# A mixer kernel on one core: the low word of float64 weights is rounded to an integer by ScalarE and added to the high part as 32-bit integers on GpSimd

## Chip, cores, metric

The program runs on one core of a Trainium2 chip. The metric is device time in microseconds (us) of one execution; lower is better. Several executions are timed and their median is given.

## What is computed

The reference chains three blocks over a batch of 8, with 576 tokens and a width of 512:

```python
# 1. attention within chunks of 64 tokens (8 heads of 64)
scores = scale * np.matmul(q_c, k_c.transpose(0, 1, 2, 4, 3))
attn = softmax(scores)                       # with the row maximum taken off
x = np.matmul(attn, v_c)
# 2. a gated block
h = np.maximum(x @ w_in, 0.0)
u, v = h[..., :512], h[..., 512:]
v_s = np.einsum('ts,bsd->btd', w_spatial, layer_norm(v)) + b_spatial[None, :, None]
x = (u * v_s) @ w_out
# 3. a token mixer and a channel mixer
u = x + (np.maximum(x^T @ w_tok1, 0.0) @ w_tok2)^T
out = u + np.maximum(u @ w_ch1, 0.0) @ w_ch2
```

Activations are float32. The weights w_in, w_out, w_tok1, w_tok2, w_ch1 and w_ch2 arrive as float64, which no engine of the kernel computes in: the kernel reads each as a pair of 32-bit words and makes a float32 of it.

## The kernel before

**Stages.** The first block and the gated block run batch by batch on PE, the tensor engine. A hand-written list of words (FIRST for the first batch, STEADY for the six that follow, LAST for the eighth) gives the order of the steps; a word is a step and the number of its tile. The second stage (token and channel mixers, from about 520 us) has its own order and converts nothing. Every engine runs its instructions strictly in the order of the list; semaphores hold an instruction until what it reads is written and its buffer is free.

**A piece of a float64 weight** has up to 128 rows and 512 columns. It is loaded by the SP queue into `craw` (two buffers; `wu_raw` for four pieces), as 32-bit words, the low word first and the high word second, so that each of them is read with a stride of 8 bytes. Then come three steps, words `wa`, `wm`, `we` for the twelve pieces of w_in and w_out in the first batch and `ca`, `cm`, `ce` for the 33 of the later weights:

- `conv_start` on ScalarE (ACT): the high word, read as a float32 and scaled, becomes `t` (tile `ctmp`, L143), and the low word, read as an integer, is scaled into a float32 in its own place (L144).
- `conv_mid` on VectorE (DVE): `t` is shifted left by three bits (L152), the sign is merged in (L154), and the power of two of the result is cut out into the place of the high word (L156).
- `conv_end` on GpSimd (POOL): low part times power of two (L164), and the product is added to `t` (L165).

After that the first twelve pieces are split into a rounded part (ACT, L187) and a rest (L190, on POOL or DVE), which the matrix products read. The 33 others are stored to memory by the SP queue (word `cs`, L215), which frees their buffers for the next loads (`cl`, L129).

**What stands around it in a steady batch.** The list has, in the early part: `x1 ca L2 S0 V0 s0 e0 ca n0 z0 cm ce V1 cm S1 R1 r1 R0 r0 ce T0 R2 r2 R3 r3 t0 V2 U0 s1 e1 P0 cs cs cl cl L3 x2 n1 z1 F G S2 ... T1`. In it `S` is the scores of a pair of heads on PE (L336), `s`, `e`, `n`, `z` their softmax (DVE L355 and L356, ACT L362, DVE L366 to L368, and the scaling on POOL, L372), `T` their transpose on PE (L380), `x` the transposes of q and k on DVE (L322, L323), `V` and `U` the product with w_in on PE (L479, L568), `R` ACT's evictions of V (L526) and `r` the batch-norm statistics on DVE (L531, L532). So two conversions stand ahead of the statistics on DVE, and behind those `s1`, `x2` and `n1`, before PE's `S2` and `T1`. Later in the batch `W` is the spatial product (L591, behind ACT's copy of the u half, L578), `D` copies the output projection out (ACT, L624) and stores it (SP, L625).

Of the kernel before, what the change touches and what calls it, by code (L numbers as in the profile page):

```python
# [10 lines left out]
U32 = mybir.dt.uint32  # L11
ACTF = mybir.ActivationFunctionType
ALU = mybir.AluOpType
# [42 lines left out]
def attention_gmlp_mixer(  # L56
# [15 lines left out]
    nc = tc.nc  # L72
# [4 lines left out]
    scale = 1.0 / float(D) ** 0.5  # L77

    def f32(ap):
        return ap.bitcast(F32)  # L80
# [34 lines left out]

    def conv_load(src, raw=None):

        nr, n = src.shape[0], src.free_size()  # L120
        if src.dtype == F32:
            raw = rp.tile([128, DM], F32, tag="ctmp", bufs=3, name="ctmp")[:nr, :n]
            nc.sync.dma_start(out=like(raw, src), in_=src)
            return raw
        if raw is None:
            raw = rp.tile([128, DM, 2], U32, tag="craw", bufs=2, name="craw")
        raw = raw[:nr, :n]
        src = src.bitcast(U32)
        nc.sync.dma_start(out=like(raw.rearrange("p n w -> p (n w)"), src), in_=src)  # L129
        return raw  # L130

    def like(ap, other):
        if len(other.shape) == 3:
            return ap.rearrange("p (g n) -> p g n", g=other.shape[1])
        return ap

    def conv_start(raw):
        if raw.dtype == F32:
            return raw, raw
        nr, n = raw.shape[:2]  # L140
        low, high = raw[:, :, 0], raw[:, :, 1]
        t = rp.tile([128, DM], F32, tag="ctmp", bufs=3, name="ctmp")[:nr, :n]
        nc.scalar.activation(out=t, in_=f32(high), func=ACTF.Copy, scale=2.0 ** -112)  # L143
        nc.scalar.activation(out=f32(low), in_=low, func=ACTF.Copy, scale=2.0 ** -52)  # L144
        return raw, t

    def conv_mid(raw, t):
        if raw.dtype == F32:
            return
        low, high = raw[:, :, 0], raw[:, :, 1]  # L150
        tu = t.bitcast(U32)
        nc.vector.tensor_scalar(  # L152
            out=tu, in0=tu, scalar1=3, scalar2=None, op0=ALU.logical_shift_left)
        nc.vector.scalar_tensor_tensor(  # L154
            out=tu, in0=high, scalar=0x80000000, in1=tu, op0=ALU.bitwise_and, op1=ALU.bitwise_or)
        nc.vector.tensor_scalar(  # L156
            out=high, in0=tu, scalar1=0xFF800000, scalar2=None, op0=ALU.bitwise_and)

    def conv_end(raw, t):

        if raw.dtype == F32:
            return raw
        low, high = raw[:, :, 0], raw[:, :, 1]
        nc.gpsimd.tensor_tensor(out=f32(high), in0=f32(low), in1=f32(high), op=ALU.mult)  # L164
        nc.gpsimd.tensor_tensor(out=t, in0=t, in1=f32(high), op=ALU.add)  # L165
        return t

    class Piece:
# [5 lines left out]
        def load(self, *a):  # L174
            self.x = conv_load(self.src, *a)

        def start(self):
            self.x = conv_start(self.x)

        def mid(self):  # L180
            conv_mid(*self.x)

        def end(self):
            self.x = conv_end(*self.x)
# [1150 lines left out]
```

## Time and profile before

| | us |
|---|---|
| median of 3 runs (lowest, highest) | 1257.33 (1256.14, 1257.96) |
| profiled execution | 1259.11 |
| its span, first to last instruction | 1257.3 |
| PE busy in the span | 1190.9 |
| DVE busy | 923.6 |
| ACT busy | 496.6 |
| POOL busy | 213.1 |

The span is that of the profiled execution; its time includes a little before the first and after the last instruction. Busy shares are averages over stages: PE is the busiest engine by far, and what an engine's waiting costs has to be read from the stage in which it waits. The rows below carry times in us from the start of the span.

### The profile page before, as it was taken

To read this page: it belongs to the slowest core of one execution; us is meant where nothing else is said; L and a number is where in the kernel's file an instruction comes from. 1 tells how busy PE (TensorE), PEld (TensorE's weight loads), DVE (VectorE), ACT (ScalarE), POOL (GpSimd) and SP (SyncE) were. 2 spreads that over 40 slices of the span, in tenths; PEclk is the share of its full clock that TensorE was granted. 3 is DMA by queue.
4 is the path that set the end of the run, shared out by engine and by line. 5 is a ranking of instruction groups with operands and counts; after the bars stand their busy time and mean duration, and the time that the engine had idled before them with its cause. 6 is when DMAs were issued, how large, how long until landed. Compare 5 with 4: busy or idle time off the path is not lost. (4 is left out here: it accounts for less than half of the span.)

```text
span 1257.3 us, 25171 instructions
## 1 busy us (share of the span) xinstructions
PE 1190.9 (95%) x9983; PEld 1123.0 (89%) x9983; DVE 923.6 (73%) x1427; ACT 496.6 (39%) x786; POOL 213.1 (17%) x205
## 2 busy tenths in 40 slices
PE   6689999999998999999889999999998999999997
PEld 4588998989797988898779899999998999999997
DVE  6897767687776868366686776767768977877786
ACT  2564535354544536244332332232225433333331
POOL 2644122222323231105220000000005100000000
PEclk9989999999999999999999999999999999999999
DMA  9956446374739383157545665565376576666663
GB/s 162 186 111 130 86 120 116 94 172 103 183 78 202 58 195 81 72 106 210 151 139 166 183 178 180 152 171 192 141 276 202 208 208 192 185 192 196 207 212 46
DMA packets 426362, 196.16 MB, mean 156 GB/s; under 512 B 369666, under 2 KB 389570, under 8 KB 426244
## 3 DMA queue, kind: packets, MB, share of 16 engines
q1 hardware_dynamic: 421380, 193.96, 58.9%
q8 instruction: 78, 1.28, 0.4%
q10 hardware_dynamic: 4864, 0.59, 0.3%
q14 instruction: 40, 0.33, 0.1%
HBM read 123.31 MB, written 71.17 MB: 155 GB/s over the span
## 5 line engine op out<-in xcount | busy, mean ns | idle before, releaser
L953 PE MATMUL ps_c<-ub,wt 128*128 128x288 f32 x2016 | 289.3, 299 | 7.8 <-DVE u L982 2.5
L953 PEld LDWEIGHTS ps_c<-ub,wt 128*128 128x128 f32 x2016 | 278.2, 191 | 14.0 <-ACT s L985 3.6
L953 PE MATMUL ps_c<-hb,wt 128*128 128x288 f32 x2016 | 269.1, 295 | 1.6 <-DVE hb L1042 1.5
L953 PEld LDWEIGHTS ps_c<-hb,wt 128*128 128x128 f32 x2016 | 268.2, 188 | 2.4 <-DVE hb L1042 2.3
L591 PE MATMUL ps_s<-ws,vn 128*128 128x288 f32 x768 | 110.9, 301 | 2.9 <-ACT ut L578 2.8
L1041 ACT CAST hb<-h 128x1728 fp32r<-128x1728 f32 x40 | 64.8, 1638 | 123.0 <-DVE h L1034 42.9
L591 PEld LDWEIGHTS ps_s<-ws,vn 128*128 128x128 f32 x768 | 105.9, 193 | 4.5 <-ACT ut L578 4.3
L617 PE MATMUL ps_o<-g,w_out 128*128 128x288 f32 x768 | 107.6, 297 | 0.7 <-DVE w_out L190 0.7
L568 PE MATMUL ps_u<-xt,w_in 128*128 128x288 f32 x768 | 107.9, 300 | 0.0
L568 PEld LDWEIGHTS ps_u<-xt,w_in 128*128 128x128 f32 x768 | 105.5, 193 | 0.9 <-POOL w_in L190 0.2
L617 PEld LDWEIGHTS ps_o<-g,w_out 128*128 128x128 f32 x768 | 102.6, 188 | 2.5 <-DVE w_out L190 0.9
L1042 DVE TENSOR_TENSOR hb<-h,hb 128x1728 fp32r<-128x1728 f32 x40 | 78.2, 1955 | 28.9 <-ACT hb L1041 28.9
L479 PE MATMUL ps_v<-w_in,xt 128*128 128x512 f32 x384 | 94.8, 404 | 2.7 <-ACT xt L423 1.3
L479 PEld LDWEIGHTS ps_v<-w_in,xt 128*128 128x128 f32 x384 | 72.8, 192 | 21.1 <-ACT xt L423 1.5
L372 POOL TENSOR_TENSOR e<-e,sm 128x512 f32<-128x512 f32 (+1 forms) x40 | 38.9, 972 | 226.9 <-DVE sm L368 153.7
L869 PE MATMUL ps_u<-w,h 128*128 128x288 f32 x384 | 61.8, 298 | 4.5 <-DVE xh L874 4.5
L910 ACT CAST ub<-xh 128x576 fp32r<-128x576 f32 x56 | 37.4, 672 | 70.0 <-DVE xh L917 66.8
L869 PEld LDWEIGHTS ps_u<-w,h 128*128 128x128 f32 x384 | 54.7, 190 | 5.7 <-DVE xh L874 5.6
L164 POOL TENSOR_TENSOR craw<-craw 128x512 f32<-128x512 f32 (+3 forms) x41 | 40.1, 978 | 116.0 <-DVE craw L156 34.0
L911 DVE TENSOR_TENSOR ub<-xh,ub 128x576 fp32r<-128x576 f32 x56 | 43.1, 770 | 21.1 <-ACT ub L910 20.6
L811 ACT CAST xn<-nat 128x512 fp32r<-128x512 f32 x40 | 24.8, 619 | 79.2 <-DVE nat L809 74.6
L830 PE MATMUL ps_h<-xn,w 128*128 128x512 f32 x192 | 51.2, 400 | 3.5 <-ACT xn L811 3.5
(145 smaller groups left out, 1697.9 us busy)
## 6 DMA issues: line engine op xcount, KB each, us to landing
hd<-c SPq DMA_DIRECT2D x120, 288.0 KB, 2.5
h<-hd SPq DMA_DIRECT2D x40, 864.0 KB, 6.7
craw<-in_moe_w_ch_dram SPq DMA_DIRECT2D x24, 512.0 KB, 4.8
x_raw<-x2d SPq DMA_DIRECT2D x160, 64.0 KB, 2.6
qk_raw<-in_q_dram SPq DMA_DIRECT2D x128, 72.0 KB, 4.2
qk_raw<-in_k_dram SPq DMA_DIRECT2D x128, 72.0 KB, 3.1
xh<-x2d SPq DMA_DIRECT2D x16, 576.0 KB, 5.6
u2d<-xh SPq DMA_DIRECT2D x16, 576.0 KB, 3.1
```

Source lines behind the costliest of these rows:

```text
L164: nc.gpsimd.tensor_tensor(out=f32(high), in0=f32(low), in1=f32(high), op=ALU.mult)
L372: nc.gpsimd.tensor_tensor(out=e, in0=e, in1=sm.to_broadcast([128, e.shape[1], 64]), op=ALU.mult)
L479: nc.tensor.matmul(ps, lhsT=self.xt[kc][:, p, 128 * ti:128 * ti + 128], rhs=w_in_t[r][:, kc, DM:2 * DM], start=kc == 0 and n == 0, stop=kc ...
L568: nc.tensor.matmul(ps[:, h, 0:HALF], lhsT=w_in_t[r][:, kc, 128 * m:128 * m + 128], rhs=self.xt[kc][:, p, HALF * h:HALF * h + HALF], start= ...
L591: nc.tensor.matmul(ps[:, h, 0:HALF], lhsT=lhsT, rhs=rhs[:, HALF * h:HALF * h + HALF], start=n == 0, stop=n == len(ops) - 1)
L617: nc.tensor.matmul(ps[:, h, 0:HALF], lhsT=w_out_t[r][:, kc, 128 * m:128 * m + 128], rhs=self.g[p][:, kc, h], start=kc == 0 and n == 0, sto ...
L830: nc.tensor.matmul(ps[kk], lhsT=PB["w1"][r][:, m, ksl], rhs=xn[:, p], start=m == 0 and n == 0, stop=False)
L869: nc.tensor.matmul(ps, lhsT=h1[:, kk, p, 128 * m:128 * m + 128], rhs=PB["w2"][r][:, kk, HALF * h:HALF * h + HALF], start=n == 0, stop=n == 5)
L911: eng.tensor_tensor(out=lo, in0=x, in1=f32(hi), op=ALU.subtract)
L953: nc.tensor.matmul(ps, lhsT=lhsT, rhs=rhs, start=first and n == 0, stop=n == len(ops) - 1, skip_group_check=True)
L1041: nc.scalar.copy(out=hi, in_=x)
L1042: nc.vector.tensor_tensor(out=lo, in0=x, in1=f32(hi), op=ALU.subtract)
```

## The change

ScalarE no longer scales the low word by 2^-52 into a float32: it scales it by 2^-29 and writes it back as a 32-bit integer, which is the number of units in the last place (0 to 8) that the low word adds to the high part's bits, rounded. DVE's third pass goes. On GpSimd the multiply goes, and in place of the float add an integer add of the bit patterns of `t` and the low word remains.

```diff
@@ conv_start
         nc.scalar.activation(out=t, in_=f32(high), func=ACTF.Copy, scale=2.0 ** -112)
-        nc.scalar.activation(out=f32(low), in_=low, func=ACTF.Copy, scale=2.0 ** -52)
+        nc.scalar.activation(out=low, in_=low, func=ACTF.Copy, scale=2.0 ** -29)
@@ conv_mid
         nc.vector.scalar_tensor_tensor(
             out=tu, in0=high, scalar=0x80000000, in1=tu, op0=ALU.bitwise_and, op1=ALU.bitwise_or)
-        nc.vector.tensor_scalar(
-            out=high, in0=tu, scalar1=0xFF800000, scalar2=None, op0=ALU.bitwise_and)
@@ conv_end
-        low, high = raw[:, :, 0], raw[:, :, 1]
-        nc.gpsimd.tensor_tensor(out=f32(high), in0=f32(low), in1=f32(high), op=ALU.mult)
-        nc.gpsimd.tensor_tensor(out=t, in0=t, in1=f32(high), op=ALU.add)
+        tu = t.bitcast(U32)
+        nc.gpsimd.tensor_tensor(out=tu, in0=tu, in1=raw[:, :, 0], op=ALU.add)
         return t
```

The order of all other instructions stays; the line numbers shift by one to two. On DVE, in a steady batch, from the first of the two conversions of the early part to the first statistics, the rows before are:

```order
L152 TENSOR_SCALAR ctmp<-ctmp 128x512
L154 SCALAR_TENSOR_TENSOR ctmp<-craw,ctmp 128x512
L156 TENSOR_SCALAR craw<-ctmp 128x512
L152 TENSOR_SCALAR ctmp<-ctmp 128x512
L154 SCALAR_TENSOR_TENSOR ctmp<-craw,ctmp 128x512
L156 TENSOR_SCALAR craw<-ctmp 128x512
L531 BN_STATS st<-v_5838 128x6
```

And now:

```order
L153 TENSOR_SCALAR ctmp<-ctmp 128x512
L155 SCALAR_TENSOR_TENSOR ctmp<-craw,ctmp 128x512
L153 TENSOR_SCALAR ctmp<-ctmp 128x512
L155 SCALAR_TENSOR_TENSOR ctmp<-craw,ctmp 128x512
L529 BN_STATS st<-v_5758 128x6
```

Two passes over 128x512 words are gone, and GpSimd's part of a piece now starts behind the second pass instead of the third. On POOL, the same place, from the softmax scaling of the first head pair to that of the second, before:

```order
L372 TENSOR_TENSOR e<-e,sm 128x512
L164 TENSOR_TENSOR craw<-craw 128x512
L165 TENSOR_TENSOR ctmp<-ctmp,craw 128x512
L164 TENSOR_TENSOR craw<-craw 128x512
L165 TENSOR_TENSOR ctmp<-ctmp,craw 128x512
L372 TENSOR_TENSOR e<-e,sm 128x512 x3
```

And now:

```order
L370 TENSOR_TENSOR e<-e,sm 128x512
L163 TENSOR_TENSOR ctmp<-ctmp,craw 128x512 x2
L370 TENSOR_TENSOR e<-e,sm 128x512 x3
```

Of four instructions between the scalings two are left, both on integers.

## Rows read from the trace of the kernel before

**Rows 1.** Page, busy time of each engine, share of the span, instructions.

```profile
PE 1190.9 (95%) x9983; PEld 1123.0 (89%) x9983; DVE 923.6 (73%) x1427; ACT 496.6 (39%) x786; POOL 213.1 (17%) x205
```

**Rows 2.** Windows: length, busy us by engine, granted clock, DMA share, GB/s.

```profile
240.00:300.00 60.00, 57.58 (x590) 53.01 (x590) 43.81 (x89) 28.88 (x54) 15.31 (x15) 1.00 0.58 130
300.00:360.00 60.00, 56.34 (x569) 51.28 (x570) 43.99 (x87) 28.57 (x52) 17.47 (x15) 1.00 0.66 155
360.00:420.00 60.00, 56.75 (x576) 52.34 (x578) 42.78 (x87) 27.11 (x51) 17.78 (x15) 0.97 0.71 154
420.00:480.00 60.00, 57.10 (x585) 52.50 (x580) 42.88 (x83) 25.92 (x51) 17.87 (x16) 0.97 0.60 142
```

**Rows 3.** Waits of PE, 125 to 560 us: total, times, longest.

```profile
PE ps_t L380 <- POOL e L372: 4.4, 4, 1.1
PE ps_s L336 <- DVE last L323: 4.4, 4, 1.8
PE ps_s L591 <- ACT ut L578: 2.8, 4, 1.1
PE ps_v L479 <- ACT x2o L624: 1.3, 1, 1.3
```

**Rows 4.** Lines of the conversion: ns of one, least/median/most, then first and last start.

```profile
L144 ACT ACTIVATE craw<-craw x41: 248/662/695, 11.4 to 514.4; 128x512 f32<-128x512 uint32 x34, 128x256 f32<-128x256 uint32 x4, 128x64 f32<-128x64 uint32 x2, 64x256 f32<-64x256 uint32 x1
L156 DVE TENSOR_SCALAR craw<-ctmp x41: 197/428/1344, 16.3 to 515.8; 128x512 uint32<-128x512 uint32 x34, 128x256 uint32<-128x256 uint32 x4, 128x64 uint32<-128x64 uint32 x2, 64x256 uint32<-64x256 uint32 x1
L164 POOL TENSOR_TENSOR craw<-craw x41: 292/1040/1432, 16.8 to 516.3; 128x512 f32<-128x512 f32 x34, 128x256 f32<-128x256 f32 x4, 128x64 f32<-128x64 f32 x2, 64x256 f32<-64x256 f32 x1
L165 POOL TENSOR_TENSOR ctmp<-ctmp,craw x41: 324/1305/1789, 17.9 to 517.4; 128x512 f32<-128x512 f32 x34, 128x256 f32<-128x256 f32 x4, 128x64 f32<-128x64 f32 x2, 64x256 f32<-64x256 f32 x1
```

**Rows 5.** Timeline, fifth batch: start, length, instruction [idle before, releaser].

```profile
326.69 2.11 ACT L526 ACTIVATE v<-ps_v 128x512 f32<-128x512 f32 x4
326.83 0.43 DVE L156 TENSOR_SCALAR craw<-ctmp 128x512 uint32<-128x512 uint32 x1
327.17 0.42 DVE L152 TENSOR_SCALAR ctmp<-ctmp 128x512 uint32<-128x512 uint32 x1
327.34 1.15 POOL L164 TENSOR_TENSOR craw<-craw 128x512 f32<-128x512 f32 x1 [1.16 <-DVE craw L156]
327.63 1.41 DVE L154 SCALAR_TENSOR_TENSOR ctmp<-craw,ctmp 128x512 uint32<-128x512 uint32 x1
328.57 1.63 POOL L165 TENSOR_TENSOR ctmp<-ctmp,craw 128x512 f32<-128x512 f32 x1
329.14 1.34 DVE L156 TENSOR_SCALAR craw<-ctmp 128x512 uint32<-128x512 uint32 x1
330.40 0.69 DVE L531 BATCH_NORM_STATS2 st<-v 128x6 f32<-128x512 f32 x1
...
336.47 1.15 PE L336 MATMUL ps_s<-qkT,qkT 64*64 64x64 f32 x32 [1.47 <-DVE last L323]
```

**Rows 6.** Timeline, seventh batch, the same place.

```profile
464.46 1.17 DVE L152 TENSOR_SCALAR ctmp<-ctmp 128x512 uint32<-128x512 uint32 x1 [0.23 <-ACT ctmp L143]
...
467.80 0.69 DVE L531 BATCH_NORM_STATS2 st<-v 128x6 f32<-128x512 f32 x1
```

**Rows 7.** Timeline of PE, end of the first batch.

```profile
109.92 0.66 PE L380 MATMUL ps_t<-ident,e 128*128 128x128 f32 x4 [0.69 <-POOL e L372]
...
111.53 3.17 PE L617 MATMUL ps_o<-g,w_out 128*128 128x288 f32 x22 [0.69 <-DVE w_out L190]
```

**Rows 8.** Timeline of the SP queue, end of the fifth batch.

```profile
372.22 0.34 SPq L215 DMA_DIRECT2D c_f<-ctmp  x1
...
380.72 5.20 SPq L625 DMA_DIRECT2D x2d<-x2o  x3
```

**Rows 9.** Groups of POOL by shape: busy us, mean ns, idle before.

```profile
L756 POOL TENSOR_TENSOR wraw<-wraw 128x256 f32<-128x256 f32 x6 | 7.0, 1173 | 0.5
```

**Rows 10.** Timeline of DVE in the first batch.

```profile
68.53 0.78 DVE L250 STREAM_TRANSPOSE ws_nat<-ws_raw 128x576 f32<-128x576 f32 x1 [0.50 <-DMA ws_raw<-in_moe_w_spatial_dram]
```

## Prediction before the run

> **What bounds the kernel now.** I began with the page's busy times: TensorE (PE) works for 1190.9 us of a span of 1257.3, VectorE (DVE) for 923.6, ScalarE (ACT) for 496.6, GpSimd (POOL) for 213.1 [rows 1]. So at most 66 us of PE idling can be won, and only where an engine that the change touches ends the wait. The conversions of float64 weights run only up to 517 us [rows 4], so I next read the windows over the batches that run in that stretch. In each of the four windows from 240 to 480 us PE idles 2.4 to 3.7 us, 12.2 us together, and in the last two the mean granted clock is 0.97 [rows 2]. Then the waits of PE from 125 to 560 us: all but nothing is left beside four groups, the transposes for POOL's softmax scaling (4.4 us, 4 times), the scores for DVE's transposes of q and k (4.4 us, 4 times), the spatial product for ACT's copy out (2.8 us) and one wait for ACT's store of the output projection (1.3 us) [rows 3]. These are the waits that a shorter conversion can reach.
>
> The timeline of one of these batches (the fifth, at 324 to 340 us) shows how they come about. Two conversions stand back to back on DVE, just ahead of the four batch-norm statistics, the softmax of the second head pair and the transposes of the third; PE's scores wait for the last of these. In that burst DVE and POOL do not overlap: the second DVE pass of 1.41 us starts at 327.63 beside POOL's multiply, which ends at 328.49, and itself ends 0.55 us later; the last pass takes 1.34 us instead of a median of 0.43, until POOL's add is through; and POOL's add, which waited in turn for DVE's pass to end at 329.04, took 1.63 us against a median of 1.30 [rows 4, 5]. The Trainium skill says the same ("SBUF — State Buffer", section "SBUF: two separate sides"): the port pair that DVE and GpSimd share is a lock held for a whole instruction, and whichever starts first makes the other wait. By that rule it could also be the add that goes first after the change; the time comes out within 0.1 us of the order that I use below, so nothing in the sum hangs on it.
>
> **What the change does to the instructions.** Per piece DVE loses its third pass (a median of 0.43 us, up to 1.34), POOL loses a multiply (1.04 us) and its float add (1.30 us) becomes an integer add on one packed and one strided operand [rows 4]. For 45 pieces (41 in these rows, seven of those shorter) that is by the medians up to 19 us on DVE and up to 47 us on POOL; almost all of it lies beside PE's work and is worth nothing. ACT keeps its two passes; the second now writes an integer. No row has ACT writing one; its pass that reads integers takes 0.662 us [rows 4], and I take that for the other direction too. ACT is 39% busy, so I put it at nothing; were it twice as long, an add and the evictions behind it would come up to 0.7 us later in each burst, 2.8 us in four.
>
> **The price of the integer add** is the unknown. Below it lies POOL's multiply of the same tile, 1.04 us; above it the costliest row per element, an add of 128x256 at 1.173 us in the mean, which for 512 columns is 2.35 us [rows 4, 9]. I take the float add that it replaces, 1.30 us: same operands, same strides, same output. A sentence by itself: the Trainium skill ("GPSIMD Engine Reference", section "Elementwise — side-by-side cycle accounting") gives 4497 ns for an add of 2048 columns, an estimate of 1.12 us for 512; with it the sum below would be larger by some 0.7 us.
>
> **The burst, worked out for the fifth batch.** Before: first DVE conversion done, its third pass starts at 326.83; statistics start at 330.40 [rows 5]. After: the second conversion's shift takes the place at 326.83 and ends at 327.25 (0.42 us, its row); the first integer add, ready since 326.83, runs from 327.27 to 328.57; the second DVE pass waits for it and ends 0.55 us behind it, as now, at 329.12; no third pass; statistics start at 329.15. That is 1.25 us earlier. ACT's four evictions, which the statistics read, end at 328.8 [rows 5], so they do not take it back. Everything behind the statistics on DVE (two softmax passes, four transposes, a sum) moves along, and PE's scores, now waiting 1.47 us, and then its transposes, waiting up to 1.1 us [rows 3, 5], lose 1.25 us between them. The fourth and sixth batch show the same pattern; I give these three 1.2 us each. In the seventh the second shift waits for ACT until 464.46, and then takes 1.17 us because POOL's multiply and add are in its way; the statistics start at 467.80 [rows 6]. After: add from 463.8 to 465.1, shift done at 465.45, second pass at 466.2: 1.6 us. In the first two steady batches PE hardly waits there (the pieces are smaller), so nothing. **Sum of the bursts: 3 x 1.2 + 1.6 = 5.2 us.**
>
> **Two smaller places.** At 109.9 and 111.5 us PE waits 0.69 us each for POOL's softmax scaling behind a conversion and for DVE's low part of the output weights [rows 7]; with a pair of 1.04 and 1.30 us cut to 1.30 on POOL and a pass less on DVE the first goes and most of the second: 1.2 us. Before that the start hides everything: DVE's transposes of the spatial weights at 68.53 us start when their DMA lands [rows 10], and the POOL and PE work up to 82 us hangs on them, so what the first eight pieces win is lost there. Once, between the fifth and sixth batch, PE waits 1.3 us for ACT [rows 3], which waits for a slot of the output tile, whose store was issued only at 380.72, since the SP queue stood before a store of converted weights until POOL's add had ended and that store went out at 372.22, with twelve loads queued between the two [rows 8]. With POOL's pair cut by 1.04 us and DVE's third pass gone that queue moves on at least 1.5 us earlier: 1.2 us.
>
> **The sum.** 5.2 + 1.2 + 1.2 = 7.6 us, from the profile's span of 1257.3 us to 1249.7 us. The profiled execution took 1259.11 us in all, 1.8 more than its span; the median of the runs is 1257.33, so I apply the 7.6 us to that: **1249.7 us**. 0.2%, or 2.5 us, is about what a measurement of this kernel can tell from no change.
>
> **Rivals.** *The integer add is slow.* Each 0.1 us of its length goes off each burst, so 5.2 us are used up when it takes 1.3 + 5.2/4 = 2.6 us, just beyond the costliest row. At 2.35 us the bursts still give 1.0, the other places about half: 1255. At 4.8 us, double the present pair, the bursts cost 14 - 5.2 = 8.8, the scaling behind the add at 109 us and the queue at 372 us 2.4 us each (4.8 less the present 2.4): about 1271. For it: no row has POOL on integers. Against it: POOL's rows cost by columns and hardly by operation (1.04 to 1.30). The Trainium skill ("GPSIMD Engine Reference", section "Engine selection") says that the cores add 32-bit integers natively, which by itself speaks for the float add's price; no row here shows it.
>
> *The time does not reach PE.* DVE is free earlier, but another wait takes over: the transposes could find their q and k not landed, or the spatial product stay where ACT's copy out lets it (2.8 us in four waits now [rows 3]). Against it: DVE goes through these transposes without a DMA wait, and ACT's copy hangs on the same DVE chain. Then only the small places count: 1255.
>
> *More than forecast.* In the windows at 0.97, PE ran at 1.2 instead of 2.4 GHz for some 2 x 0.06 x 60 = 7.2 us in all behind the two stalls and lost about half of that, 3.6 us [rows 2]. Shorter stalls might leave the clock up: 1246. Against it: where it stayed up, in the fourth and fifth batch, PE lost up to 1.1 us again at the spatial product, since ACT was not ready; that wait is part of the 2.8 us [rows 3]. So I count nothing.
>
> **How the numbers follow.** Forecast (1247 to 1252.5): 0.60. Add between 2 and 2.6 us (1254 to 1257): 0.08; add slower than that: 0.10. Time that does not reach PE (1254 to 1257): 0.12. Clock stays up (1244 to 1247): 0.10. The low end at 1246 takes in a good part of the last, the high end at 1256.5 most of the second and fourth; outside remain the slow add and the tips. Faster by over 0.2% (below 1254.8): 0.60 + 0.10 and a little of the others, 0.72; slower by over 0.2%: 0.11; within: 0.17.
>
> **What the next profile would show.** POOL's one row per piece at about 1.3 us for 128x512 (the first thing to look at); DVE's second pass still stretched in the bursts but the statistics 1.2 to 1.6 us nearer to it; PE's waits for DVE's transposes and POOL's scaling down from 8.8 to some 4 us; the wait for ACT's store gone; idle of the windows of the four batches from 12 to about 6 us; windows before 80 us unchanged. The prediction falls if the add takes over 2.3 us, or if the four waits shrink and waits for ACT's copy out or for DMAs grow by as much.

## The result and the profile after

The changed kernel takes 1243.72 us (median of 4 runs, 1242.73 to 1245.07), the kernel before 1257.43 in the same comparison (4 runs, 1256.14 to 1257.96): ratio 0.9889, 95% interval 0.9875 to 0.9903. That is 13.7 us less where 7.6 were forecast, and 2.3 us below the low end of the range (1246.0). The profiled executions have spans of 1243.1 and 1257.3 us; that of the changed kernel is the longest of its four.

The page of the changed kernel, busy time of each engine, answers to [rows 1]:

```profile
PE 1189.7 (96%) x9983; PEld 1121.2 (90%) x9983; DVE 888.2 (71%) x1382; ACT 496.7 (40%) x786; POOL 167.6 (13%) x160
```

DVE is 35 us and POOL 45 us lighter, ACT the same; hardly any of that is PE's time. Three lines of the conversion (the first two give least/median/most ns of one, the third busy us, mean ns and the idle time before), to be held against [rows 4]:

```profile
L145 ACT ACTIVATE craw<-craw x41: 248/659/686, 10.7 to 499.5; 128x512 uint32<-128x512 uint32 x34, 128x256 uint32<-128x256 uint32 x4, 128x64 uint32<-128x64 uint32 x2, 64x256 uint32<-64x256 uint32 x1
L155 DVE SCALAR_TENSOR_TENSOR ctmp<-craw,ctmp x41: 226/693/1679, 15.1 to 500.1; 128x512 uint32<-128x512 uint32 x34, 128x256 uint32<-128x256 uint32 x4, 128x64 uint32<-128x64 uint32 x2, 64x256 uint32<-64x256 uint32 x1
L163 POOL TENSOR_TENSOR ctmp<-ctmp,craw 128x512 uint32<-128x512 uint32 x34 | 45.0, 1324 | 93.2 <-DVE ctmp L155 68.5 <-ACT aT L386 8.1 <-DMA x2d<-x2o 6.2
```

The two unknown prices came out as taken: the integer add at 1.32 us is the float add, and ACT's pass that writes integers, 0.659 us, is the one that wrote floats. So the instructions cost what the prediction gave them; the surplus lies elsewhere.

The windows of the four middle batches, columns as in [rows 2]:

```profile
240.00:300.00 60.00, 59.69 (x623) 55.30 (x623) 43.53 (x89) 29.19 (x50) 11.45 (x10) 1.00 0.59 144
300.00:360.00 60.00, 57.97 (x595) 53.50 (x594) 41.06 (x85) 29.57 (x54) 11.58 (x11) 1.00 0.59 137
360.00:420.00 60.00, 58.76 (x627) 54.05 (x626) 41.98 (x85) 29.12 (x54) 12.13 (x10) 1.00 0.68 159
420.00:480.00 60.00, 59.33 (x593) 54.92 (x592) 42.25 (x88) 30.87 (x57) 11.19 (x10) 1.00 0.63 141
```

PE's idle time there falls from 12.2 to 4.3 us (the forecast said about 6), and the granted clock is 1.00 throughout. The waits of PE, 125 to 560 us, against [rows 3]:

```profile
PE ps_s L589 <- ACT ut L576: 3.8, 6, 1.1
PE ps_t L378 <- POOL e L370: 1.1, 2, 1.0
```

The waits for DVE's transposes and for ACT's store are gone, those for POOL's scaling are a quarter of what they were.

**Where the time came from.** The start of PE's first product with w_in (V) marks each batch in both traces. The second batch starts at 117.48 instead of 120.25 us, 2.8 us earlier. From there to the start of the eighth it is 388.48 instead of 400.54 us, 12.1 less, all of it in the fourth to seventh batch. The second stage gives 0.6 back. 2.8 + 12.1 - 0.6 = 14.3, against a difference of the spans of 14.2.

The fifth batch after, DVE, POOL and PE, is the burst of [rows 5]; its first V product on PE starts at 310.79:

```profile
319.26 0.38 DVE L153 TENSOR_SCALAR ctmp<-ctmp 128x512 uint32<-128x512 uint32 x1
319.67 1.43 DVE L155 SCALAR_TENSOR_TENSOR ctmp<-craw,ctmp 128x512 uint32<-128x512 uint32 x1
321.03 0.41 DVE L153 TENSOR_SCALAR ctmp<-ctmp 128x512 uint32<-128x512 uint32 x1
321.24 1.36 POOL L163 TENSOR_TENSOR ctmp<-ctmp,craw 128x512 uint32<-128x512 uint32 x1 [0.68 <-DMA qk_raw<-in_k_dram]
321.48 1.68 DVE L155 SCALAR_TENSOR_TENSOR ctmp<-craw,ctmp 128x512 uint32<-128x512 uint32 x1
323.07 0.68 DVE L529 BATCH_NORM_STATS2 st<-v 128x6 f32<-128x512 f32 x1
...
329.34 1.10 PE L334 MATMUL ps_s<-qkT,qkT 64*64 64x64 f32 x32
...
331.40 0.44 PE L378 MATMUL ps_t<-ident,e 128*128 128x128 f32 x2 [0.96 <-POOL e L370]
```

From the start of the second shift to the first statistics it is now 2.04 us; before, from the start of the third pass in its place, 3.57 (326.83 to 330.40). The add starts 0.14 us behind the first merge, while DVE shifts; the second merge is stretched to 1.68 us and ends 0.56 us behind the add. PE's scores no longer wait.

But the burst is not only shorter. Counted from the batch's first V product, this is where it starts (first shift) and where the first statistics start, in us, for the fourth to seventh batch, and how long the batch lasts to the next first V product:

| | first shift | first statistics | length of the batch |
|---|---|---|---|
| before | 7.40, 8.67, 8.04, 8.51 | 12.92, 14.19, 13.56, 14.46 | 67.08, 69.42, 67.71, 67.45 |
| after | 4.66, 8.47, 7.69, 6.64 | 8.88, 12.28, 11.51, 10.86 | 64.38, 66.19, 65.39, 63.59 |

From first shift to statistics the four bursts are 1.30, 1.71, 1.70 and 1.73 us shorter, 6.4 together; and they start 2.74, 0.20, 0.35 and 1.87 us earlier, 5.2 together. The second of these the prediction did not have. Its size is that of one pair of traces. In a second trace of the changed kernel (experiment 7) the bursts start at 4.61, 7.15, 4.49 and 7.60, together 8.8 us earlier than before, and are 6.2 us shorter; and where the later pieces are converted as before (first part of experiment 5) they start at 6.30, 8.03, 8.02 and 7.97, 2.3 us earlier in all without any change there. So the start moves by a few us from trace to trace, while the shortening stays.

**Why the burst starts earlier.** In the seventh batch, before, the SP queue (the first four rows), ACT (the next two) and POOL (the last) read as follows; the first V product starts at 453.34:

```profile
439.86 0.34 SPq L215 DMA_DIRECT2D c_f<-ctmp  x1
...
449.52 4.03 SPq L625 DMA_DIRECT2D x2d<-x2o  x3
453.67 0.35 SPq L215 DMA_DIRECT2D c_f<-ctmp  x1
454.07 0.45 SPq L129 DMA_DIRECT2D craw<-in_moe_w_ch_dram  x1
...
452.57 0.64 ACT L624 COPY x2o<-ps_o 128x576 f32<-128x576 f32 x1 [5.17 <-DMA x2d<-x2o]
...
459.04 0.66 ACT L143 ACTIVATE ctmp<-craw 128x512 f32<-128x512 f32 x1 [4.18 <-DMA craw<-in_moe_w_ch_dram]
...
438.53 1.31 POOL L165 TENSOR_TENSOR ctmp<-ctmp,craw 128x512 f32<-128x512 f32 x1
```

The first conversion of the batch (ACT, 459.04) waits for a load that SP issues only at 454.07, 0.73 us behind the V product. SP stood until then at the stores of the output tile (`x2d<-x2o`), of which the third waits for ACT's copy at 452.57, which itself waits for the slot that the first of these stores frees. Behind that conversion, on ACT, stands the exponential of the first head pair, and behind the exponential, on DVE, the sum and the first shift. So a late SP queue sets the start of the next burst. The same rows after, with the first V product at 442.37:

```profile
426.64 0.34 SPq L213 DMA_DIRECT2D c_f<-ctmp  x1
...
434.93 5.64 SPq L623 DMA_DIRECT2D x2d<-x2o  x3
440.67 0.38 SPq L213 DMA_DIRECT2D c_f<-ctmp  x1
441.14 0.41 SPq L130 DMA_DIRECT2D craw<-in_moe_w_ch_dram  x1
...
439.58 0.64 ACT L622 COPY x2o<-ps_o 128x576 f32<-128x576 f32 x1 [3.16 <-DMA x2d<-x2o]
...
446.20 0.66 ACT L144 ACTIVATE ctmp<-craw 128x512 f32<-128x512 f32 x1 [4.12 <-DMA craw<-in_moe_w_ch_dram]
...
425.31 1.31 POOL L163 TENSOR_TENSOR ctmp<-ctmp,craw 128x512 uint32<-128x512 uint32 x1 [0.68 <-DVE ctmp L155]
```

The stores come 7.44 us ahead of the V product instead of 3.82, the load 1.23 us ahead instead of 0.73 behind, the conversion 3.83 behind instead of 5.70: 1.87 us earlier, which is what the first shift gains. That the queue is ahead begins with the conversion at the end of the batch before: the first row of each fence is a store of converted weights, which goes out when POOL's add has ended (439.84 before, 426.62 after), 13.48 us ahead of the V product before and 15.73 after. These are 2.25 us of the 3.62 by which the stores of the output tile come earlier; the rest lies at the loads of v that stand between them (2.41 us before, 0.99 after).

### The profile page after: what moved, and what is told of

The parts are those of the page before. It is cut to its first block, busy times and chain, and to the rows that moved or that the text cites. A ratio compares the mean times of both kernels' runs of the same rounds, so it can differ in the third digit from the quotient of the medians.

```text
span 1243.1 us, 25025 instructions
## 1 busy us (share of the span) xinstructions
PE 1189.7 (96%) x9983; PEld 1121.2 (90%) x9983; DVE 888.2 (71%) x1382; ACT 496.7 (40%) x786; POOL 167.6 (13%) x160
## 3 DMA queue, kind: packets, MB, share of 16 engines
q8 instruction: 78, 1.28, 0.4%
## 5 line engine op out<-in xcount | busy, mean ns | idle before, releaser
L163 POOL TENSOR_TENSOR ctmp<-ctmp,craw 128x512 uint32<-128x512 uint32 (+3 forms) x41 | 49.4, 1205 | 117.5 <-DVE ctmp L155 81.7
```

The costliest lines, as they stand in the source:

```text
L163: nc.gpsimd.tensor_tensor(out=tu, in0=tu, in1=raw[:, :, 0], op=ALU.add)
```

## The experiments

Each run stands beside runs of the kernel before on the same chip, whose medians lie between 1256.27 and 1257.37 us; the ratios are to those.

**1. The changed kernel with DVE's third pass put back**, its result read by nothing.

```diff
             out=tu, in0=high, scalar=0x80000000, in1=tu, op0=ALU.bitwise_and, op1=ALU.bitwise_or)
+        nc.vector.tensor_scalar(
+            out=high, in0=tu, scalar1=0xFF800000, scalar2=None, op0=ALU.bitwise_and)
```

> The changed kernel with VectorE's third pass put back (its result is read by nobody). Theory A: the time went two ways: the burst of two conversions ahead of the statistics became shorter on VectorE (1.7 us from the end of the first merge to the statistics in the fifth to seventh batch), and it starts earlier (up to 2.7 us in the fourth and 1.9 us in the seventh batch), since GpSimd ends each piece earlier, so that the SP queue's stores and the next loads behind them go out earlier. By it this kernel keeps the early loads and loses about half of the burst: two passes of 0.43 us and some waiting beside the add, 0.9 to 1.3 us in each of four batches, so 4 to 5 us slower than the changed kernel, about 1248. Theory B: only VectorE's time counts; then nearly all is lost, 1254 or more. Theory C: only GpSimd's time counts; then 1244.

Measured: 1244.63 us (1243.25 to 1251.14), ratio 0.9923 [0.9896, 0.9950].

**2. The changed kernel with a multiply on POOL** ahead of the integer add, its result read by nothing.

```diff
+        high = f32(raw[:, :, 1])
+        nc.gpsimd.tensor_tensor(out=high, in0=high, in1=high, op=ALU.mult)
         nc.gpsimd.tensor_tensor(out=tu, in0=tu, in1=raw[:, :, 0], op=ALU.add)
```

> The changed kernel with a GpSimd multiply of 128x512 put back ahead of each integer add (the high words times themselves, read by nobody). Theory A: the burst on VectorE is hardly longer, for the second merge waits behind a multiply of 1.04 us where it now waits behind an add of 1.30; but stores and loads go out 1 us and more later, so the start of the burst in the fourth and seventh batch goes back by up to 2.7 and 1.9 us and the wait for the store of the output projection returns: 4 to 6 us slower than the changed kernel, about 1249. Theory B (only VectorE's time counts): 1244, as the changed kernel. Theory C (only GpSimd's time counts): all is lost, 1256.

Measured: 1246.28 us (1245.64 to 1249.19), ratio 0.9934 [0.9910, 0.9958]. With the one or the other pass back, 0.77% or 0.66% of the 1.11% remain; the interval of experiment 1 overlaps that of the changed kernel, so that the DVE pass by itself costs anything is not shown. The forecast by bursts (some 1248 and 1249) took too much away in both. In the two traces the four bursts still start 9.9 and 5.0 us earlier than before, in all, and are 3.0 and 3.8 us shorter.

**3. Both passes put back**, with the wait of before between them.

```diff
+        nc.vector.tensor_scalar(
+            out=high, in0=tu, scalar1=0xFF800000, scalar2=None, op0=ALU.bitwise_and)
@@ conv_end
+        high = f32(raw[:, :, 1])
+        nc.gpsimd.tensor_tensor(out=high, in0=high, in1=high, op=ALU.mult)
         nc.gpsimd.tensor_tensor(out=tu, in0=tu, in1=raw[:, :, 0], op=ALU.add)
```

> The changed kernel with both removed passes put back: DVE's third pass writes the power of two into the high word, and POOL multiplies the high words with themselves ahead of the integer add (that result is read by nothing; the output is unchanged). Each piece has again the five instructions of before, in the order of before, but ScalarE's integer write and the integer add stay. Theory A (all of the gain is the two passes and the wait between them, the integer forms themselves are worth nothing): the time of before, about 1257 us, the first statistics about 13 to 14 us behind the batch's first V product. Theory B (a part of the gain comes from the integer forms, for instance because the integer add does not hold DVE up as the float pair does): 1252 us or less.

Measured: 1255.50 us (1253.05 to 1256.35, 11 runs), ratio 0.9982 [0.9973, 0.9991]. So the two passes are all but 0.18% of the gain. Counted from here, leaving out the DVE pass alone (experiment 2) gives 0.48%, the multiply alone (experiment 1) 0.59%, and both 0.93%: within the intervals they add up. DVE and POOL in the fifth batch show the burst of before again, on integers (first V product at 314.90):

```profile
325.28 0.43 DVE L157 TENSOR_SCALAR craw<-ctmp 128x512 uint32<-128x512 uint32 x1
325.62 0.42 DVE L153 TENSOR_SCALAR ctmp<-ctmp 128x512 uint32<-128x512 uint32 x1
325.79 1.15 POOL L166 TENSOR_TENSOR craw<-craw 128x512 f32<-128x512 f32 x1 [1.16 <-DVE craw L157]
326.08 1.41 DVE L155 SCALAR_TENSOR_TENSOR ctmp<-craw,ctmp 128x512 uint32<-128x512 uint32 x1
326.90 1.75 POOL L167 TENSOR_TENSOR ctmp<-ctmp,craw 128x512 uint32<-128x512 uint32 x1
327.59 1.35 DVE L157 TENSOR_SCALAR craw<-ctmp 128x512 uint32<-128x512 uint32 x1
328.86 0.68 DVE L533 BATCH_NORM_STATS2 st<-v 128x6 f32<-128x512 f32 x1
```

3.58 us from the third pass to the statistics, as in [rows 5]. Why 0.18% remain is not settled; here the add does not read the multiply's result, and a pair on POOL is about 0.1 us shorter for it (0.11 to 2.41 us against 0.66 to 3.09 from the first V product of the fourth batch).

**4. A third DVE pass that POOL's add waits for**, and no multiply.

```diff
             out=tu, in0=high, scalar=0x80000000, in1=tu, op0=ALU.bitwise_and, op1=ALU.bitwise_or)
+        nc.vector.tensor_scalar(
+            out=tu, in0=tu, scalar1=0xFFFFFFFF, scalar2=None, op0=ALU.bitwise_and)
```

> The changed kernel with a third DVE pass that rewrites t itself (an AND with all ones), so that POOL's add waits for the third pass as POOL's multiply did before; POOL keeps its one add. Beside the run with a third pass that nothing waits for (0.9923 of before) it tells apart: theory A (the gain of either removal alone is nearly the whole, because POOL's part then starts beside the next shift and not behind a third pass): about 1250 us or more, first statistics 12 to 13 us behind the first V product. Theory B (the length of POOL's part is what counts, the wait does not): as the run with the unread third pass, 1245 to 1247 us.

Measured: 1244.30 us (1243.60 to 1247.98), ratio 0.9905 [0.9891, 0.9919]. That the add no longer waits for a third pass is worth nothing that shows: experiment 1 has the pass without the wait, at 0.9923, and the intervals overlap. The theory that the wait is what matters falls.

**5. The change for the first batch's twelve pieces alone, and for the 33 later ones alone.** A flag `new` goes through the three steps:

```diff
-        nc.scalar.activation(out=f32(low), in_=low, func=ACTF.Copy, scale=2.0 ** -52)
+        if new:
+            nc.scalar.activation(out=low, in_=low, func=ACTF.Copy, scale=2.0 ** -29)
+        else:
+            nc.scalar.activation(out=f32(low), in_=low, func=ACTF.Copy, scale=2.0 ** -52)
```

First batch alone:

> The change for the twelve pieces of the first batch alone; the 33 later ones are converted as before. Theory A: the product with V of the second batch starts 2.8 us earlier, as it does in the changed kernel, and the later batches gain nothing: 1254.6. What is open is how these 2.8 us come about: 1.4 from the two waits at 110 us, and 1.8 from TensorE not running its spatial product at the lower clock. If the clock part is chance, 1256.

Later pieces alone:

> The change for the 33 later pieces alone; the twelve of the first batch as before. Theory A: 10.0 us in the four bursts and 2.1 us at the ends of the batches, less some 0.6 that the second stage gives back: 1246. If the two halves add up, this and the kernel with the first twelve alone gain together what the whole change gains, 13.7 us.

Measured: 1254.03 us, ratio 0.9979 [0.9966, 0.9991], and 1243.85 us, ratio 0.9901 [0.9874, 0.9928]. The parts, 0.21% and 0.99%, add up to the whole, 1.11%, within their intervals; in us they are about 2.6 and 12.4, where 1.2 and 6.4 were forecast.

**6. The exponential ahead of the conversion on ACT**, in the kernel before and in the changed one. In the words of a steady batch:

```diff
-x1 ca L2 S0 V0 s0 e0 ca n0 z0 cm ce V1 cm S1 R1 r1 R0 r0 ce T0 R2 r2 R3 r3 t0 V2 U0 s1 e1
+x1 L2 S0 V0 s0 e0 ca n0 z0 ca cm ce V1 cm S1 R1 r1 R0 r0 ce T0 R2 r2 R3 r3 t0 V2 U0 s1 e1
```

In the kernel before:

> The kernel before, with nothing changed but the place of two words of the steady order: ScalarE's first conversion step stands behind the exponential of the first head pair instead of ahead of it, and the second behind the scaling. In the fifth batch before, ScalarE stood 4.9 us for the load of that piece with the exponential behind it, though the scores were ready 1.5 us before. Theory A (the start of the burst hangs on that load, through ScalarE): the softmax goes ahead, only the conversions wait; the statistics come 1.5 to 2.6 us earlier in each of four batches, and 6 to 10 us are won without any work removed: about 1249. Theory B (the amount of work on VectorE): no gain, 1257.

In the changed kernel:

> The changed kernel with the same two words moved. In the fifth batch of its trace ScalarE still stands 5.0 us for the load, with the exponential behind it, and TensorE still waits 4.9 us in all from 120 to 520 us. Theory A: most of the 1.1 us for the scaling and part of the 3.8 us for ScalarE's copy out goes, 2 to 4 us: about 1241. If that copy out is held by something else in the batch, no gain: 1244.

Measured: 1252.19 us, ratio 0.9965 [0.9952, 0.9979], and 1242.94 us, ratio 0.9900 [0.9872, 0.9928]. In the kernel before that is 4.4 us, less than the 6 to 10 expected. There the first shift now starts at 4.9 to 6.7 us, but the second conversion then waits 2.8 to 4.3 us for its own load, and the statistics still start at 12.0 to 13.2. The exponential was one link of the chain; the load behind it is the other. Where that load stands in its queue is the question of experiment 8.

**7. The changed kernel, and the changed kernel with the words of experiment 6, once more, side by side.**

> The changed kernel as it is, once more, for a comparison on the same chip with the three others: 1243 to 1245 us.

> The changed kernel with ScalarE's two conversion starts behind the first softmax exponential, once more beside the changed kernel itself. If the earlier exponential is worth something (the last 2.0 us of waits for ACT at the spatial product go, as in the one profile): 1240 to 1241 us, 0.2 to 0.3% under the changed kernel. If batches are already bound by PE: the same as the changed kernel.

Measured: 1242.31 us (1240.05 to 1248.45), ratio 0.9889 [0.9872, 0.9907], and 1240.91 us (1240.87 to 1242.02), ratio 0.9872 [0.9858, 0.9886]. The second is the lower, but the intervals overlap.

By then twelve traces had the start of the statistics and the length of the batch for the fourth to seventh batch each, and they lie on one line: a batch lasts 64.4 us (63.2 for the seventh), plus what its first statistics come later than 10.45 us behind its first V product. This went into the expectations of experiment 8.

**8. The load no longer behind the late store.** One word, D2 (the third copy out of the output projection and its store), moves behind the next conversion start on ACT and behind the store and load of that stretch on SP. The instructions of the conversion stay.

```diff
-cs cs cl cl L5 W3 P3 T4 M3 H3 J3 A0 A1 B0 t4 B1 p3 q3 D0 ca x4 P4 D1 cm O2 p4 q4 ce D2 ca
-O3 cs cl cm ce D3 cs cl
+cs cs cl cl L5 W3 P3 T4 M3 H3 J3 A0 A1 B0 t4 B1 p3 q3 D0 ca x4 P4 D1 cm O2 p4 q4 ce ca
+O3 cs cl D2 cm ce D3 cs cl
```

In the kernel before:

> The kernel before, with one word of its list moved: the third copy out of the output projection (D2) stands behind ScalarE's third conversion start and behind the store and load of that stretch, so that these no longer wait for a slot of the output tile, whose first store stands late in the SP queue. The conversion keeps its five instructions. Theory A (in the batches from the fourth on the burst ahead of the statistics starts late because the next load is issued behind that store; each batch lasts a floor of 64.4 us, 63.2 for the last, plus whatever the first statistics come later than 10.45 us behind the first V product): the load is issued 2 to 4 us earlier against the first V product, the first shift starts some 2 us earlier, first statistics at 11 to 12.5 us, and the time falls by 5 to 9 us, to 1248 to 1252. Theory B (the start of the burst hangs on something else, for instance on the conversion's own length): same as before, 1255 us or more.

In the changed kernel:

> The changed kernel with the same word moved. Theory A: of the 3.2 us that its batches still last over the floor (statistics at 12.3, 11.5 and 10.9 us) most goes: 1240 to 1242 us, where the changed kernel takes 1242.3 to 1243.7. Theory B: no difference.

Measured: 1247.82 us (1246.80 to 1248.36), ratio 0.9921 [0.9907, 0.9934], and 1241.29 us (1241.02 to 1241.48), ratio 0.9871 [0.9857, 0.9884]. In the kernel before that is 9.9 us, with no pass removed. Its SP queue and ACT in the seventh batch, whose first V product starts at 446.28:

```profile
443.31 0.41 SPq L215 DMA_DIRECT2D c_f<-ctmp  x1
443.76 0.59 SPq L129 DMA_DIRECT2D craw<-in_moe_w_ch_dram  x1
...
445.26 0.64 ACT L624 COPY x2o<-ps_o 128x576 f32<-128x576 f32 x1 [3.77 <-DMA x2d<-x2o]
...
449.47 0.67 ACT L143 ACTIVATE ctmp<-craw 128x512 f32<-128x512 f32 x1 [2.74 <-DMA craw<-in_moe_w_ch_dram]
```

The load is issued 2.5 us ahead of the V product instead of 0.7 behind, and the conversion starts at 3.2 instead of 5.7. Over the four batches the first shift starts at 4.21, 5.52, 4.54 and 6.01, the statistics at 10.16, 11.09, 10.16 and 11.69, with the burst itself as long as ever (5.6 to 6.0 us); the batches last 64.68, 65.82, 64.66 and 64.67. So the start of the burst is a lever of its own, in the kernel before larger than the shortening, and it hangs on the place of that load. The move also takes ACT's last conversion start of the batch out from behind D2's copy, which no run separates; but what ACT waits for ahead of the burst's first conversion is still that load (2.74 us in the last row). In the changed kernel all four batches are at the floor (64.40, 64.39, 64.41, 63.23), and there is no more to be had at this place: 1241.3 and, in experiment 7, 1240.9 us are the two lowest medians of all runs, and neither is shown apart from the changed kernel's.

Of the 56 batches of the 14 traces, 50 lie within 0.3 us of that line. The other six are 0.56 below to 1.63 above it. In the three furthest above, the fifth batch of the kernel before (1.28), of experiment 6 in the kernel before (1.63) and of experiment 5's first part (0.85), PE's next V product waits 1.3, 1.6 and 0.5 us for ACT's copy, the wait that [rows 3] shows once.

## Why the prediction was wrong

The direction stood, and so did the mechanism as far as it went, shorter bursts that PE waits for; the sum was short by 6.6 us of span. By its terms, in us, from the one pair of traces:

| term | forecast | measured |
|---|---|---|
| up to the second batch | 1.2 | 2.8 |
| four bursts, shorter | 5.2 | 6.4 |
| four bursts, earlier start | 0 | 5.2 |
| the part of both that PE cannot use (fourth batch, 10.45 - 8.88) | 0 | -1.6 |
| the wait for ACT's store, and the rest | 1.2 | 2.1 |
| second stage | 0 | -0.6 |
| sum | 7.6 | 14.3 |

**The price of the integer add** was right: 1.32 us for 1.30 taken. ACT's integer write at nothing was right (0.659 us for 0.662), and so was that the second batch gains nothing (64.50 us to the third before, 64.53 after).

**The step that failed** is "the sum of the bursts: 3 x 1.2 + 1.6 = 5.2 us". It timed a burst from its own start and held that start where it was. The start is set by a load that SP issues behind a store, and that queue had fallen behind because the conversions of the batch's end held it. I had read that very queue [rows 8] and priced it, but only at the one wait of PE that it ends, 1.2 us; its larger part is the next batch's burst, 5.2 us in this pair of traces, 8.8 with the second trace after. Experiment 8 shows the lever by itself: the load put elsewhere is worth 9.9 us in the kernel before.

**The burst's length** was mis-sized by little, 6.4 for 5.2 us. In the fifth batch I gave 2.32 us from the second shift to the statistics (326.83 to 329.15), and it took 2.04. I let the first integer add start behind DVE's shift and take its full 1.30 us from there. Its record begins 0.20 us ahead of the shift's end, and the add ends 1.16 us behind the shift (321.44 to 322.60), just as POOL's add in [rows 5] ends 1.16 us behind DVE's second pass; the remaining 0.12 us lie at the statistics, whose record begins 0.09 us ahead of the merge's end and not behind it. The Trainium skill ("SBUF — State Buffer", section "SBUF: two separate sides") has the exclusive lock of the shared ports held by a DVE instruction with two inputs from SBUF or in a two-port mode. The trace after agrees for the merge, which has two (at 321.48 it takes 1.68 us for a median of 0.69). The shift has one input, and the add shuts it out as well: in the seventh batch after, where the add starts first, the shift takes 1.28 us for a median of 0.40 and ends 0.29 us behind the add. Whether the shift runs in a two-port mode no run here shows. So the prediction's use of the rule for the shift was right.

```profile
450.99 1.31 POOL L163 TENSOR_TENSOR ctmp<-ctmp,craw 128x512 uint32<-128x512 uint32 x1 [0.68 <-DMA qk_raw<-in_q_dram]
451.31 1.28 DVE L153 TENSOR_SCALAR ctmp<-ctmp 128x512 uint32<-128x512 uint32 x1 [0.45 <-ACT ctmp L144]
```

**The smaller places.** Both waits of 0.69 us [rows 7] are gone. Most of the rest of the first 2.8 us, some 0.9 us, lies at 82 us, where I had put nothing. The transposes there come no earlier after than before (81.14 against 80.68), though PE's wait for POOL's scaling ahead of them is 1.47 instead of 2.70 us; but the products behind them run at full clock, and the next 24 start at 87.03 instead of 87.95. First the kernel before, then, in a second fence, after:

```profile
80.68 1.11 PE L380 MATMUL ps_t<-ident,e 128*128 128x128 f32 x4 [2.70 <-POOL e L372]
81.91 5.68 PE L591 MATMUL ps_s<-ws,vn 128*128 128x288 f32 x24
```

```profile
81.14 0.66 PE L378 MATMUL ps_t<-ident,e 128*128 128x128 f32 x4 [1.47 <-POOL e L370]
82.36 3.85 PE L589 MATMUL ps_s<-ws,vn 128*128 128x288 f32 x24 [0.57 <-ACT ut L576]
```

The granted clock from 82 to 86 us was 0.50 before, half speed, and 1.00 after. This place differs between executions of the same instructions (the second batch starts at 119.03 to 122.18 us in four traces that have the old conversion in the first batch and the old order ahead of it, and at 116.22 to 118.50 in six that have the change in the first batch and nothing added to it), so 2.8 us is the size of one pair of traces; the timed 2.6 us of experiment 5 say the same.

**The rivals.** The slow add did not come. "The time does not reach PE" fell: the waits for ACT at the spatial product went from 2.8 to 3.8 us and took no more than that. "More than forecast" named the right side with a wrong reason for the batches: the clock did stay up in the last two windows, but the sixth and seventh batch of the kernel before, with a mean clock of 0.97 there, lie 0.20 and 0.24 us off the line, as does its fourth (0.21) at 1.00. PE at half speed cost nothing there, for the reason that the prediction gave against this rival. The half speed falls behind the statistics (in the sixth batch the mean granted clock from 407 to 412 us is 0.66, and the statistics start at 399.2), on the 72 products with the u half of w_in, which take 11.01 us where they take 9.82 in the fifth; the fifth batch, at full speed, then waits 1.07 us for ACT at the spatial product, and the sixth does not wait there:

```profile
339.14 9.82 PE L568 MATMUL ps_u<-xt,w_in 128*128 128x288 f32 x72
...
352.17 3.46 PE L591 MATMUL ps_s<-ws,vn 128*128 128x288 f32 x24 [1.07 <-ACT ut L578]
...
408.10 11.01 PE L568 MATMUL ps_u<-xt,w_in 128*128 128x288 f32 x72
...
421.00 3.43 PE L591 MATMUL ps_s<-ws,vn 128*128 128x288 f32 x24
```

What stays open: the 0.18% of experiment 3, by how much the first batch's clock differs from run to run, and what part of the gain the earlier start has on average, since it differs between the traces.

## What to carry to other kernels

An interval that gets shorter is half of a forecast; the other half is what sets its start. Follow that back one batch, through the in-order queues, before holding it fixed: here the burst's start hung on a load, the load on a store ahead of it in the queue, and the store on the end of the previous conversions, so what was saved at one end of a batch came back at the start of the next.

In a loop that repeats, plot the length of the round against the time of the event that its slowest wait hangs on, over whatever traces there are: a floor and a slope of one tell at once what a microsecond earlier is worth, and from where on it is worth nothing.

## What the hardware showed that was not expected

- A GpSimd add of two 128x512 operands as 32-bit integers takes 1.32 us in the mean, one of them read with a stride of 8 bytes, as the float add did (median 1.305).
- The add holds up DVE's single-input shift as it does the two-input merge: the shift took 1.28 us and ended 0.29 us behind the add, the merge took 1.68 us and ended 0.56 us behind it. Where the shift starts first, the records overlap by 0.20 us, but the add ends 1.16 us behind the shift. The statistics beside the second add (0.66 to 0.68 us from 323.07 on) were not held up.
- A lower granted clock need not cost time: at 0.97 and at 1.00 in the mean the batches lie on the same line, since the 1.2 us that half speed cost took the place of a wait of 1.07 us; while in the first batch 24 products took 5.68 us, at 0.50 for the most part, and 3.85 at 1.00, directly on the path.
